# Three reorderings in a fused retention, mixture-of-experts and token-mixing kernel: weight loads, attention transposes, edge channel products

## The chip, the cores and the metric

The kernel runs on one core of one Trainium2 chip. The metric is the device time of one execution in microseconds (us). TensorE is called PE below, VectorE DVE, ScalarE ACT, GpSimd POOL, and SyncE, which issues nearly all transfers, SP.

## The reference

Eight batches of 576 tokens and 512 channels (8 heads of 64) pass three layers in float32.

```
scores = scale * q @ k.T ; ret = scores * gamma_h ** (i - j) for i >= j ; x = ret @ v          # retention
logits = x @ w_gate ; the best 2 of 4 experts, softmax over these two                         # gate
out   += w_e * (softmax(causal(scale * (x wq_e) @ (x wk_e).T)) @ (x wv_e) @ wo_e)             # per expert
theta  = x @ w_theta ; zr = x cos(theta) ; zi = x sin(theta)
u      = x + w_tok_r @ zr + w_tok_i @ zi                                                      # token mixing
result = u + max(u @ w_ch, 0)                                                                 # channel product
```

## The kernel before

Products whose operands need more than one PE pass are split into a high and a low part (`split`: ACT writes the high part, DVE the low one) and multiplied in three passes (`mm3`, lines 102 to 104).

**Start, 0 to 45 us.** The retention of batch 0 runs chunk by chunk (128 tokens) through `ret_step`: scores of a chunk (L144), a running state `pS` (L160, copied to SBUF by ACT as `S`, L163), values (L173 and L180), then `xt` (DVE), `xh` (ACT) and `xl` (POOL). `vp` (L129, POOL) scales V of a chunk and waits for that chunk's `kv` transfer. The projections of the experts need `w1`, 512 rows of 772 columns: Q and K in columns 0 to 512, V and the gate in 512 to 772. SP loads it as four blocks of rows, ahead of the chunks 1 to 3 of `kt` and `kv`, and each block is split whole into `WH` and `WL` (L435) behind chunk 0's `xt`. The first projection, `v0` (`proj_v`, L259), multiplies columns 512 to 772 of all four blocks. PE runs 50 matmuls on zeros before the first data and 40 more (`WARM2`) ahead of `v0`.

**Attention, 45 to 475 us.** The units (batch, pair of experts p, row tile m of 5) go through a loop in which the order on PE is written by hand (`manual_schedule`); the other engines' order is a scheduler's. Each batch has ten slots, table `SLOTS`; the last batch has `LAST`. A slot t issues: `at_scores` of unit t (L321; DVE takes the minimum, L324, and ACT the exponential `P`, L329), the projections that the table names, in slot 1 the products of V that are due ("O"), then `at_trans` of unit t-1 (L368: PE transposes `P`, DVE copies one expert's transpose to `PT`, ACT the other's, L373 and L375), and in five slots one `ret_step` of the next batch ("R1" to "R5"). Inside a `ret_step`, behind 12 groups of its values, `mid` issues the due products of V (`at_out`, L387), which read `PT`; what follows is the state of the next chunk, which writes `pS` again and so waits until ACT has copied `S`. All PSUM tiles of this phase but `pS` share one pool of 7 buffers, `w`.

**Mixing, 475 to 891 us.** Here the scheduler orders all engines. `mix(b, h)` multiplies 108 matmuls into the channel half h of batch b (L750), with the sines and products of `z_tile` (L599 to L608) as operands, which DVE and ACT prepare ahead. When a half is done, DVE adds x to it (L762; in batch 0, where x came in by transposes, it only copies, L764) and so frees the PSUM tiles `acc`; ACT and DVE or POOL split it to `uh`, `ul` (L765, L766). `channel(b, et)` multiplies four k tiles of `uh`, `ul` into one block of 128 output channels (2 column halves of 288, 12 matmuls each, 24 per block), of which k tiles 0 and 1 come from `mix(b, 0)`, 2 and 3 from `mix(b, 1)`. Four or five `token_tile`s for the coming batches (12 matmuls each, 512 wide; ACT L582, L584, DVE L585, L587) stand behind the halves. `x_put` (DVE L793, four SP transfers) writes x of later batches transposed to DRAM, `x_get` reads it back as `u`.

Of the kernel before, what the change touches and what calls it, by code (L numbers as in the profile page):

```python
# [10 lines left out]
F32 = mybir.dt.float32  # L11
# [5 lines left out]
OP = mybir.AluOpType  # L17
# [3 lines left out]
B, H, S, D = 8, 8, 576, 64  # L21
E, DM = 4, 512
C = 128
# [4 lines left out]
NW1 = 2 * 2 * 128 + NV  # L28
# [5 lines left out]
TH = [(0, 288), (288, 576)]  # L34
# [14 lines left out]
WARM2 = 40  # L49
# [13 lines left out]
def tile_kernel(ctx: ExitStack, tc: tile.TileContext, qk, kv, w1, wo, wot, wd, cst, out):  # L63
# [42 lines left out]
    def split(h, l, src):  # L106
        nc.scalar.activation(h, src, AF.Copy)  # L107
        MARK["split"] = nc.vector.tensor_sub(l, src, h)  # L108
# [318 lines left out]
    wst = []  # L427

    def load_w1(kt):
        st = w1s.tile([128, NW1], F32, name="wst", bufs=4)  # L430
        nc.sync.dma_start(st, w1[kt * 128:(kt + 1) * 128, :])
        wst.append(st)

    def split_w1(kt):
        split(WH[:, kt, :], WL[:, kt, :], wst[kt])  # L435

    for kt in range(4):
        load_w1(kt)
    for c in range(1, LDB):
        loads(0, c)  # L440
    with tc.issue_after(MARK["pool"].ins):
        nc.gpsimd.dma_start(cm, cst[:, o:o + 1088])
# [74 lines left out]
    for kt in range(4):  # L517
        with tc.issue_after(MARK["xt"].ins), tc.issue_after(MARK["xh" if kt > 1 else "S"].ins):
            split_w1(kt)
# [7 lines left out]
    scale()  # L527
    with tc.issue_after(MARK["sm"].ins):
        make_gt(2)
    ret_step(0, 1, (0, 2))  # L530
    for c in range(3, NCH):
        with tc.issue_after(MARK["xt"].ins):
            make_gt(c)
    w1s.release()
    ret_step(0, 2, (0, 3))
# [91 lines left out]
    outs = []  # L627
    for t in range(nu + 1):
        b, k = divmod(t, 10)
        if b < B - 1:  # L630
            more, between, after = *SLOTS[k], ""
        else:
            b = B - 1
            more, between, after = LAST[t - 10 * b]
        if t < nu:
            at_scores(units[t])
            work(b, more)
            if units[t][2] == NCH - 1:
                at_norm(*units[t][:2])
# [5 lines left out]
        if between == "O":  # L645
            for o in outs:
                at_out(*o)
            outs = []
        if t:
            at_trans(units[t - 1])  # L650
            ub, up, um = units[t - 1]
            if GROUPS[GRP[um]][-1] == um:
                outs.append((ub, up, GRP[um]))
        if b < B - 1:
            if between[:1] == "R":
                c = int(between[1])
                x = b + 1
                def mid():
                    for o in outs:
                        at_out(*o)  # L660
                    outs.clear()

                ret_step(x, c - 1, (x, c) if c < NCH else (x + 1, 0) if x + 1 < B else None, mid)
        else:
            work(b, between)
            for o in outs:
                at_out(*o)
            outs = []
# [42 lines left out]
    def mix(b, h):  # L711
# [7 lines left out]
        for i in tiles:  # L719
            if w == 0 or i != 4:  # L720
                z_tile(g, i, h)
# [36 lines left out]
        for d in range(2):  # L758
# [7 lines left out]
            (nc.vector if h else nc.gpsimd).tensor_sub(ul[:, k, :], u[:, k, :], uh[:, k, :])  # L766

    TAIL = {}
    EDGE = (0, B - 1)

    def channel(b, et):
# [3 lines left out]
        for j, (t0, t1) in enumerate(TH):  # L775
            spare = b in EDGE
            ps = ps2.tile([128, t1 - t0], F32, name=f"acc{et % 2}{j}" if spare else "w", bufs=1 if spare else 4,
                          padded_shape=[128, 512])
# [4 lines left out]
            if b == B - 1:  # L783
                nc.sync.dma_start(out[b, et, :, t0:t1], o)
        if b < B - 1:
            nc.sync.dma_start(out[b, et], u[:, et, :])
# [28 lines left out]
    for b in range(B):  # L815
# [20 lines left out]
        for et in range(4):  # L836
            channel(b, et)
            for x in q[2 * et:2 * et + 2] if not b else []:
                x_put(*x)
# [85 lines left out]
```

## Time and profile before

| | us |
|---|---|
| median of 3 runs (lowest, highest) | 894.57 (894.08, 895.03) |
| the profiled execution | 893.5 |
| its span, first to last instruction | 891.2 |
| PE busy in the span | 862.5 (97%) |
| DVE, ACT, POOL busy | 618.1, 465.8, 219.8 |

Busy time counts matmuls whose ends are modelled. In a row of a timeline the first number is the start, the second the length of the instruction or group, and the bracket at the end the idle time of that engine just before it and what released it. "issue" stands for idle time in which the engine waited for nothing that the profile shows.

### The profile page before, as it was taken

Reading aid. Unit: us, or ns where it says so; the run is one execution under the profiler, and the core shown is the slowest. Engines: PE = TensorE matmul, PEld = TensorE weight load, DVE = VectorE, ACT = ScalarE, POOL = GpSimd, SP = SyncE. Lnnn points to the kernel's source line nnn. Section 1 sums busy time; section 2 is a strip of 40 time slices with the busy share of each in tenths; the row PEclk is TensorE's granted clock in tenths of the full one; section 3 lists DMA queues with packets and bytes.
Section 4 is the critical chain, followed back from the end, with each engine's and each line's share of the span. In section 5 each row is a group of like instructions: output and inputs, shape, how many; then the busy total and the mean of one; then the engine's idle time right before and its main releaser. Section 6 shows DMA issues by size and latency. Waiting matters only on the chain.

```text
span 891.2 us, 25579 instructions
## 1 busy us (share of the span) xinstructions
PE 862.5 (97%) x10102; PEld 802.8 (90%) x10102; DVE 618.1 (69%) x1707; ACT 465.8 (52%) x1270; POOL 219.8 (25%) x268
## 2 busy tenths in 40 slices
PE   7899999999999999999999899999999999999998
PEld 6898989888898889988778899999999999999998
DVE  3387778878777886877767946966477764776632
ACT  3375666666666666666666613544245533445320
POOL 2325153443535444342300112010120101101010
PEclk9999999999999999999999999999999999999999
DMA  9758676676857667637795252334426124251311
GB/s 321 230 144 248 160 216 178 190 232 178 245 154 209 192 189 228 165 101 219 218 300 153 33 137 52 67 88 102 121 51 140 33 72 107 37 130 25 86 46 53
DMA packets 147126, 130.28 MB, mean 146 GB/s; under 512 B 84032, under 2 KB 122688, under 8 KB 147008
## 3 DMA queue, kind: packets, MB, share of 16 engines
q1 hardware_dynamic: 146864, 128.39, 52.3%
q8 instruction: 79, 1.29, 0.6%
q0 software_dynamic: 144, 0.28, 0.2%
q14 instruction: 39, 0.32, 0.1%
HBM read 78.03 MB, written 32.00 MB: 123 GB/s over the span
## 4 chain that ended last, share of the span: by engine, by line
PE 80%; DVE 11%; ACT 2%; DMA 2%; issue 2%; SPq 1%; POOL 0%; DVEq 0%; ACTq 0%; POOLq 0%
PE acc L750 21%; PE w L102 10%; PE w L104 10%; PE w L103 10%; PE w L321 5%; PE w L259 5%; PE w L387 5%; PE w L368 3%; PE pS L160 3%; PE w L750 2%; PE w L144 1%; DVE b L462 1%; DVE P L324 1%; PE w L180 1%; PE acc L102 1%
## 5 line engine op out<-in xcount | busy, mean ns | idle before, releaser
L750 PE MATMUL acc<-TK,zh 128*128 128x288 f32 (+2 forms) x896 | 155.9, 296 | 0.5 <-ACT ob L391 0.5
L750 PEld LDWEIGHTS acc<-TK,zh 128*128 128x128 f32 x896 | 131.9, 189 | 0.8 <-issue 0.6
L329 ACT ACTIVATE P<-P,st 128x128 f32<-128x128 f32 (+4 forms) x160 | 95.6, 598 | 43.1 <-DVE st L324 42.9
L750 PE MATMUL acc<-TK,zl 128*128 128x288 f32 (+1 forms) x448 | 95.8, 295 | 0.0
L766 POOL TENSOR_TENSOR ul<-u,uh 128x576 fp32r<-128x576 f32 x16 | 24.3, 1535 | 285.2 <-ACT uh L765 285.2
L324 DVE CUSTOM_DVE_ANT_0 P<-w,cm 128x128 f32<-128x128 f32 (+4 forms) x160 | 72.0, 477 | 10.4 <-PE w L321 10.1
L321 PE MATMUL w<-KK,U 128*64 128x288 f32 (+4 forms) x384 | 76.6, 327 | 0.3 <-issue 0.2
L102 PE MATMUL w<-xh,WH 128*128 128x288 f32 x256 | 75.9, 297 | 0.5 <-issue 0.5
L104 PE MATMUL w<-xh,WL 128*128 128x288 f32 x256 | 75.4, 295 | 0.0
L103 PE MATMUL w<-xl,WH 128*128 128x288 f32 x256 | 75.3, 294 | 0.0
L750 PEld LDWEIGHTS acc<-TK,zl 128*128 128x128 f32 x448 | 72.4, 189 | 0.0
L107 ACT ACTIVATE zh<-cs 128x512 fp32r<-128x512 f32 x64 | 40.3, 630 | 59.7 <-PE acc L750 43.6
L108 DVE TENSOR_TENSOR zl<-cs,zh 128x512 fp32r<-128x512 f32 x64 | 44.1, 689 | 37.3 <-ACT zh L107 36.7
L193 POOL TENSOR_TENSOR xl<-xt,xh 128x512 fp32r<-128x512 f32 (+1 forms) x40 | 48.7, 1219 | 82.5 <-ACT xh L192 74.6
L601 ACT ACTIVATE cs<-cs,quarter 128x256 f32<-128x256 f32 x72 | 36.4, 506 | 60.3 <-DVE cs L599 56.1
L604 DVE SCALAR_TENSOR_TENSOR cs<-cs,x 128x512 f32<-128x512 f32 x72 | 49.3, 687 | 19.9 <-ACT cs L602 19.1
L387 PE MATMUL w<-PT,V 128*64 128x192 f32 (+3 forms) x576 | 56.2, 325 | 6.4 <-DVE PT L373 4.9
L466 POOL TENSOR_TENSOR r<-r,ex 128x192 f32<-128x192 f32 (+1 forms) x51 | 29.4, 576 | 130.1 <-ACT hl L467 51.1
L321 PEld LDWEIGHTS w<-KK,U 128*128 128x128 f32 (+1 forms) x384 | 53.9, 171 | 6.8 <-issue 2.3
L368 PE MATMUL w<-ident,P 128*128 128x128 f32 (+2 forms) x480 | 59.0, 258 | 0.0
L387 PEld LDWEIGHTS w<-PT,V 128*64 128x64 f32 (+1 forms) x576 | 35.6, 135 | 24.3 <-DVE PT L373 6.5
L104 PE MATMUL w<-uh,CH 128*128 128x288 f32 x192 | 56.6, 295 | 0.0
(160 smaller groups left out, 2393.1 us busy)
## 6 DMA issues: line engine op xcount, KB each, us to landing
KK<-KN SPq DMA_DIRECT2D x128, 144.0 KB
kt<-qk SPq DMA_DIRECT2D x32, 512.0 KB
kv<-kv SPq DMA_DIRECT2D x32, 512.0 KB
raw<-wd SPq DMA_DIRECT2D x43, 192.0 KB
xd<-xb SPq DMA_DIRECT2D x126, 64.0 KB
out<-u SPq DMA_DIRECT2D x28, 288.0 KB
u<-xd SPq DMA_DIRECT2D x28, 288.0 KB
td<-hl SPq DMA_DIRECT2D x27, 192.0 KB
```

What stands on the lines that cost most here:

```text
L102: nc.tensor.matmul(ps, ah, bh, start=first, stop=False)
L103: nc.tensor.matmul(ps, ah, bl, start=False, stop=False)
L104: nc.tensor.matmul(ps, al, bh, start=False, stop=last)
L193: MARK["xl"] = nc.gpsimd.tensor_sub(xl[:, :, cs], xt, xh[:, :, cs])
L259: nc.tensor.matmul(ps[:R], x[:, kt, cs], W[:, kt, w0:w0 + NV], start=x is xh and W is WH and kt == 0, stop=x is xl and kt == 3)
L321: nc.tensor.matmul(ps[s][:R], U[:, s, rs], KK[:, s, x, j0:j1], start=x == 0, stop=x == 1)
L324: MARK["dve"] = nc.vector.tensor_tensor_reduce(Ps[s][:R, j0:j1], ps[s][:R], cm[:R, o + j0:o + j1], 1.0, st[:R, 0, s:s + 1] if i else 3.0e3 ...
L329: MARK["act"] = nc.scalar.activation(Ps[s][:R, :n], Ps[s][:R, :n], AF.Exp, bias=st[:R, last, s:s + 1], scale=-1.0, accum_out=SUM[p][:R, m, ...
L368: nc.tensor.transpose(tp[:w, j, :], Ps[s][:R, j * C:j * C + w], ident[:R, :R])
L387: nc.tensor.matmul(po[s * 64:s * 64 + 64, c0:], V[:ROWS[j], j, 2 * p + s, :], v, start=j == 0, stop=j == last, skip_group_check=True)
L604: nc.vector.scalar_tensor_tensor(z, cs, -1.0, x2[:, None, ds].to_broadcast([128, 2, 256]), op0=OP.mult, op1=OP.mult)
L750: nc.tensor.matmul(acc[d][j], A[:, dc], TK[:, kt, W, t0:t1], start=q == 0 and n == 0, stop=q == 8 and n == 2)
```

## The change

`w1` comes in two transfers: columns 512 to 772 (V and gate) of all four row blocks ahead of the chunks 1 to 3, columns 0 to 512 (Q and K) behind them. V's part is split in two pieces ahead of `v0`, Q's and K's in four pieces behind the retention step of chunk 2. `WARM2` goes from 40 to 10, and the load of the mask `cm` on POOL's queue goes behind the `vp` of a later chunk. In the attention loop `at_trans` of unit t-1 stands ahead of `at_scores` of unit t; in the slots with "R2" it goes into `mid` of that `ret_step`. In the first and the last batch `channel2` takes two blocks of output channels at once: the 24 matmuls on k tiles 0 and 1 of both, then the 24 on k tiles 2 and 3. In batch 0 `x_put` and in batch 1 the first half's `z_tile`s are issued behind the last `ul` of the half before (`MARK["u"]`).

```diff
@@ -46,7 +46,7 @@
          ("v0", "R3"), ("v1", ""), ("v2 k00", "R4"), ("q00", "R5"), ("v3 k01 v4 g", "")]
 PTV = (0,)
 WARM = 50
-WARM2 = 40
+WARM2 = 10
 WB = 7
 JOBS = (58, 75)
 
@@ -424,22 +424,21 @@
         R = ROWS[c]
         nc.vector.tensor_mul(gt[:, :, c * C:c * C + R], gt[:, :, :R], gf[:, :, c, None].to_broadcast([128, 4, R]))
 
-    wst = []
-
-    def load_w1(kt):
-        st = w1s.tile([128, NW1], F32, name="wst", bufs=4)
-        nc.sync.dma_start(st, w1[kt * 128:(kt + 1) * 128, :])
-        wst.append(st)
-
-    def split_w1(kt):
-        split(WH[:, kt, :], WL[:, kt, :], wst[kt])
-
-    for kt in range(4):
-        load_w1(kt)
+    wst = {}
+
+    def load_w1(a, z):
+        wst[a] = w1s.tile([128, 4, z - a], F32, name=f"wst{a}", bufs=1)
+        nc.sync.dma_start(wst[a], w1.rearrange("(k p) n -> p k n", p=128)[:, :, a:z])
+
+    def split_w1(a, k):
+        t = wst[a]
+        sl = slice(a, a + t.shape[2])
+        split(WH[:, k, sl], WL[:, k, sl], t[:, k])
+
+    load_w1(512, NW1)
     for c in range(1, LDB):
         loads(0, c)
-    with tc.issue_after(MARK["pool"].ins):
-        nc.gpsimd.dma_start(cm, cst[:, o:o + 1088])
+    load_w1(0, 512)
     nc.sync.dma_start(tie, cst[:, o + 1088:o + 1088 + E * E].rearrange("p (a b) -> p a b", a=E))
     nc.sync.dma_start(ident, cst[:, 0:128])
 
@@ -514,9 +513,9 @@
 
     ret_step(0, -1, (0, 0))
     ret_step(0, 0, None)
-    for kt in range(4):
-        with tc.issue_after(MARK["xt"].ins), tc.issue_after(MARK["xh" if kt > 1 else "S"].ins):
-            split_w1(kt)
+    for k in range(2):
+        with tc.issue_after(MARK["xt"].ins), tc.issue_after(MARK["xh" if k else "S"].ins):
+            split_w1(512, slice(2 * k, 2 * k + 2))
     with tc.issue_after(MARK["xl"].ins):
         scale()
     warm_up(WARM2)
@@ -525,14 +524,19 @@
         make_gt(1)
     ret_step(0, -1, (0, 1))
     scale()
+    with tc.issue_after(MARK["pool"].ins):
+        nc.gpsimd.dma_start(cm, cst[:, o:o + 1088])
     with tc.issue_after(MARK["sm"].ins):
         make_gt(2)
     ret_step(0, 1, (0, 2))
     for c in range(3, NCH):
         with tc.issue_after(MARK["xt"].ins):
             make_gt(c)
+    ret_step(0, 2, (0, 3))
+    for k in range(4):
+        with tc.issue_after(MARK["xt"].ins), tc.issue_after(MARK["xh"].ins):
+            split_w1(0, k)
     w1s.release()
-    ret_step(0, 2, (0, 3))
     work(-1, "v1")
     ret_step(0, 3, (0, 4))
     work(-1, "v2 k00")
@@ -625,6 +629,13 @@
     njobs = [len(x) for x in jobs]
     due = [(JOBS[0] - 2) / njobs[0], (JOBS[1] - JOBS[0]) / njobs[1]]
     outs = []
+
+    def trans(i):
+        at_trans(units[i])
+        ub, up, um = units[i]
+        if GROUPS[GRP[um]][-1] == um:
+            outs.append((ub, up, GRP[um]))
+
     for t in range(nu + 1):
         b, k = divmod(t, 10)
         if b < B - 1:
@@ -632,6 +643,10 @@
         else:
             b = B - 1
             more, between, after = LAST[t - 10 * b]
+        n0 = len(outs)
+        late = b < B - 1 and between == "R2"
+        if t and not late:
+            trans(t - 1)
         if t < nu:
             at_scores(units[t])
             work(b, more)
@@ -643,19 +658,17 @@
             atk.release()
             zp = pool("zp")
         if between == "O":
-            for o in outs:
+            for o in outs[:n0]:
                 at_out(*o)
-            outs = []
-        if t:
-            at_trans(units[t - 1])
-            ub, up, um = units[t - 1]
-            if GROUPS[GRP[um]][-1] == um:
-                outs.append((ub, up, GRP[um]))
+            del outs[:n0]
         if b < B - 1:
             if between[:1] == "R":
                 c = int(between[1])
                 x = b + 1
                 def mid():
+                    if late:
+                        trans(t - 1)
+                        return
                     for o in outs:
                         at_out(*o)
                     outs.clear()
@@ -718,7 +731,10 @@
         ks = []
         for i in tiles:
             if w == 0 or i != 4:
-                z_tile(g, i, h)
+                with ExitStack() as es:
+                    if b == 1 and not h:
+                        es.enter_context(tc.issue_after(MARK["u"].ins))
+                    z_tile(g, i, h)
             if w == 0 and i == 4:
                 TAIL[g, h] = ZT[g, 4, h]
             if i == 4:
@@ -763,27 +779,44 @@
                 else:
                     nc.vector.tensor_copy(u[:, k, t0:t1], acc[d][j])
             nc.scalar.activation(uh[:, k, :], u[:, k, :], AF.Copy)
-            (nc.vector if h else nc.gpsimd).tensor_sub(ul[:, k, :], u[:, k, :], uh[:, k, :])
+            MARK["u"] = (nc.vector if h else nc.gpsimd).tensor_sub(ul[:, k, :], u[:, k, :], uh[:, k, :])
 
     TAIL = {}
     EDGE = (0, B - 1)
+
+    def channel2(b, ets):
+        uh, ul = UT[b]
+        u = XU[b]
+        ps = {}
+        for h in range(2):
+            for et in ets:
+                es = slice(et * C, et * C + C)
+                for kt in (2 * h, 2 * h + 1):
+                    for j, (t0, t1) in enumerate(TH):
+                        if not kt:
+                            ps[et, j] = ps2.tile([128, t1 - t0], F32, name=f"acc{et % 2}{j}", bufs=1,
+                                                 padded_shape=[128, 512])
+                        mm3(ps[et, j], CH[:, kt, 0, es], CH[:, kt, 1, es], uh[:, kt, t0:t1], ul[:, kt, t0:t1],
+                            kt == 0, kt == 3)
+                for j, (t0, t1) in enumerate(TH if h else []):
+                    o = u[:, et, t0:t1]
+                    MARK["ch"] = nc.vector.scalar_tensor_tensor(o, ps[et, j], 0.0, o, op0=OP.max, op1=OP.add)
+                    if b == B - 1:
+                        nc.sync.dma_start(out[b, et, :, t0:t1], o)
+                if h and b < B - 1:
+                    nc.sync.dma_start(out[b, et], u[:, et, :])
 
     def channel(b, et):
         uh, ul = UT[b]
         u = XU[b]
         es = slice(et * C, et * C + C)
         for j, (t0, t1) in enumerate(TH):
-            spare = b in EDGE
-            ps = ps2.tile([128, t1 - t0], F32, name=f"acc{et % 2}{j}" if spare else "w", bufs=1 if spare else 4,
-                          padded_shape=[128, 512])
+            ps = ps2.tile([128, t1 - t0], F32, name="w", bufs=4, padded_shape=[128, 512])
             for kt in range(4):
                 mm3(ps, CH[:, kt, 0, es], CH[:, kt, 1, es], uh[:, kt, t0:t1], ul[:, kt, t0:t1], kt == 0, kt == 3)
             o = u[:, et, t0:t1]
             MARK["ch"] = nc.vector.scalar_tensor_tensor(o, ps, 0.0, o, op0=OP.max, op1=OP.add)
-            if b == B - 1:
-                nc.sync.dma_start(out[b, et, :, t0:t1], o)
-        if b < B - 1:
-            nc.sync.dma_start(out[b, et], u[:, et, :])
+        nc.sync.dma_start(out[b, et], u[:, et, :])
 
     XU = {}
 
@@ -833,10 +866,15 @@
                 x_put(*x)
         if 0 < b < B - 1:
             x_get(b + 1)
-        for et in range(4):
-            channel(b, et)
-            for x in q[2 * et:2 * et + 2] if not b else []:
-                x_put(*x)
+        if b not in EDGE:
+            for et in range(4):
+                channel(b, et)
+            continue
+        for i in range(2):
+            channel2(b, (2 * i, 2 * i + 1))
+            with tc.issue_after(MARK["u"].ins):
+                for x in q[4 * i:4 * i + 4] if not b else []:
+                    x_put(*x)
         if not b:
             x_get(1)
     ps2.release()
```

Where this puts instructions, at three places. The first is PE in slot 8 ("q00", "R5") of a batch: U and KK are Q and K of the unit, xh, xl, WH, WL belong to the projection q00, kt to the retention scores, PT and V to the products of V. Before:

```order
L321 MATMUL w<-KK,U 128x512 x4
L102 MATMUL w<-xh,WH 128x288
...
L368 MATMUL w<-ident,P 128x128 x6
L144 MATMUL w<-kt 64x64 x2
...
L387 MATMUL w<-PT,V 64x256 x4
L387 MATMUL w<-PT,V 64x128 x2
```

and with the change:

```order
L368 MATMUL w<-ident,P 128x128 x6
L321 MATMUL w<-KK,U 128x512 x4
L102 MATMUL w<-xh,WH 128x288
...
L144 MATMUL w<-kt 64x64 x2
...
L387 MATMUL w<-PT,V 64x256 x4
L387 MATMUL w<-PT,V 64x128 x2
```

The six transposes stood between the projection and the retention step whose middle reads their copies; now the scores and the projection lie between as well.

The second is DVE at the end of `mix(0, 1)`: cs, zh, zl, ztl belong to `z_tile`, x to the token tiles, the w read by COPY are the PSUM tiles of the mix. Before:

```order
L793 STREAM_TRANSPOSE xb<-x_8959 128x512
L604 SCALAR_TENSOR_TENSOR cs<-cs,x_8918 128x512
L604 SCALAR_TENSOR_TENSOR cs<-cs,x_8959 128x512
L108 TENSOR_TENSOR zl<-cs,zh 128x512
L599 TENSOR_SCALAR cs<-nr 128x256
L600 TENSOR_SCALAR cs<-nr 128x256
L108 TENSOR_TENSOR zl<-cs,zh 128x512
L764 COPY u<-w 128x256
```

and with the change:

```order
L608 SCALAR_TENSOR_TENSOR cs<-cs,x_8731 128x512
L108 TENSOR_TENSOR ztl<-cs,zth 64x256 x4
L780 COPY u<-w 128x256
L780 COPY u<-w 128x320
L780 COPY u<-w 128x256
L780 COPY u<-w 128x320
L782 TENSOR_TENSOR ul<-u,uh 128x576 x2
L826 STREAM_TRANSPOSE xb<-x_8731 128x512
```

The copies of u stood behind work for batch 1; now they follow the last operands of `mix(0, 1)` itself, and the transposes of x for batch 1 come after them.

The third is DVE at the end of `mix(1, 0)`: the acc are its PSUM tiles, k and nr belong to a token tile, u is batch 1's x, read back by `x_get`. Before:

```order
L604 SCALAR_TENSOR_TENSOR cs<-cs,x_8959 128x512
L108 TENSOR_TENSOR zl<-cs,zh 128x512
L762 TENSOR_TENSOR u<-acc_9537,u 128x288
L762 TENSOR_TENSOR u<-acc_9538,u 128x288
L762 TENSOR_TENSOR u<-acc_9539,u 128x288
```

and with the change:

```order
L589 TENSOR_SCALAR k<-k 128x512
L591 TENSOR_TENSOR nr<-k,w 128x512
L589 TENSOR_SCALAR k<-k 128x512
L591 TENSOR_TENSOR nr<-k,w 128x512
L778 TENSOR_TENSOR u<-acc_9507,u 128x288
L778 TENSOR_TENSOR u<-acc_9508,u 128x288
L778 TENSOR_TENSOR u<-acc_9509,u 128x288
```

The adds that free the tiles stood behind `z_tile` work; now they stand behind the k and nr of the fourth token tile, since PE's order has four token tiles (before: two) between `mix(1, 0)` and `mix(1, 1)`.

## Rows read from the trace of the kernel before

**Rows 1.** The page: busy time by engine, the chain by engine, one costly group.

```profile
PE 862.5 (97%) x10102; PEld 802.8 (90%) x10102; DVE 618.1 (69%) x1707; ACT 465.8 (52%) x1270; POOL 219.8 (25%) x268
...
L387 PE MATMUL w<-PT,V 128*64 128x192 f32 (+3 forms) x576 | 56.2, 325 | 6.4 <-DVE PT L373 4.9
```

**Rows 2.** Stretches of the span: us long, busy by engine (instructions), granted clock, DMA share, GB/s.

```profile
0.00:20.00 20.00, 15.77 (x342) 14.37 (x346) 8.01 (x11) 6.73 (x12) 6.24 (x15) 1.00 0.93 321
20.00:45.00 25.00, 20.25 (x460) 19.02 (x452) 7.75 (x17) 7.54 (x21) 8.36 (x9) 1.00 0.79 233
45.00:475.00 430.00, 417.19 (x6482) 373.96 (x6481) 333.36 (x1116) 280.97 (x886) 164.49 (x223) 1.00 0.68 196
```

**Rows 3.** What PE waited for: total us, times, longest.

```profile
PE pS L160 <- ACT S L163: 7.1, 11, 0.8
...
PE w L180 <- issue: 2.2, 2, 1.4
PE w L144 <- issue: 1.6, 1, 1.6
```

**Rows 4.** Timeline of PE, 9 to 18 us: start, us, operation, [idle before <-releaser].

```profile
16.00 0.65 PE L259 MATMUL w<-WH,xl 128*128 128x260 f32 x4
```

**Rows 5.** Timeline of DVE, 9 to 18 us.

```profile
11.06 4.66 DVE L108 TENSOR_TENSOR WL<-wst,WH 128x772 fp32r<-128x772 f32 x4
```

**Rows 6.** Timeline of POOL, 9 to 30 us.

```profile
16.56 1.04 POOL L129 TENSOR_TENSOR vp<-kv,gam 128x512 f32<-128x512 f32 x1 [2.53 <-DMA kv<-kv]
```

**Rows 7.** DMA of the first 50 us: one queue's packets, MB, share.

```profile
q8 instruction: 6, 0.10, 0.7%
```

**Rows 8.** Timeline of PE, 61 to 66 us (slot 4).

```profile
60.68 1.04 PE L368 MATMUL w<-ident,P 128*128 128x128 f32 x8
...
63.98 0.27 PE L160 MATMUL pS<-vp,kv 64*64 64x64 f32 x2 [0.70 <-ACT S L163]
```

**Rows 9.** Timeline of ACT, 61 to 66 us (slot 4).

```profile
62.99 0.56 ACT L373 COPY PT<-w 128x512 f32<-128x512 f32 x1
63.45 0.38 ACT L163 ACTIVATE S<-pS 128x256 f32<-128x256 f32 x1
```

**Rows 10.** Timeline of PE, 84 to 419 us (slot 8; last batch).

```profile
85.01 1.08 PE L387 MATMUL w<-PT,V 128*64 128x256 f32 x8 [0.43 <-DVE PT L373]
...
418.50 0.49 PE L387 MATMUL w<-PT,V 128*64 128x128 f32 x4 [1.41 <-DVE PT L373]
```

**Rows 11.** Timeline of PE and ACT, 228 to 234 us (slot 6).

```profile
230.33 0.64 PE L259 MATMUL w<-WH,xl 128*128 128x260 f32 x4
...
230.72 0.49 ACT L329 ACTIVATE P<-P,st 128x256 f32<-128x256 f32 x1
```

**Rows 12.** Timeline of PE and DVE, 503 to 516 us (first batch's channel product).

```profile
505.97 0.30 PE L102 MATMUL acc<-uh,CH 128*128 128x288 f32 x1
...
506.90 0.29 PE L103 MATMUL acc<-ul,CH 128*128 128x288 f32 x1
510.79 0.61 PE L102 MATMUL acc<-uh,CH 128*128 128x288 f32 x1 [3.60 <-ACT uh L765]
...
506.06 1.25 DVE L604 SCALAR_TENSOR_TENSOR cs<-cs,x 128x512 f32<-128x512 f32 x2
...
509.20 1.55 DVE L764 COPY u<-w 128x256 f32<-128x256 f32 x4
```

**Rows 13.** Stretch of the same place, PE alone: us, busy (instructions), granted clock.

```profile
510.25:513.70 3.45, 2.91 (x12) 0.51 0.00 0
```

**Rows 14.** Groups of 520 to 640 us: busy us, mean ns of one | idle before.

```profile
L762 DVE TENSOR_TENSOR u<-acc,u 128x288 f32<-128x288 f32 x16 | 6.4, 448 | 11.3 <-PE acc L750 11.3
...
L585 DVE TENSOR_SCALAR k<-k 128x512 f32<-128x512 f32 x9 | 6.3, 697 | 1.3 <-ACT k L584 1.2
L587 DVE TENSOR_TENSOR nr<-k,w 128x512 f32<-128x512 f32 x9 | 6.2, 683 | 0.2
...
L584 ACT ACTIVATE k<-w 128x512 f32<-128x512 f32 x9 | 5.3, 586 | 1.9 <-DVE nr L587 1.1 <-PE w L104 0.8
```

## The prediction

> **What bounds the kernel now.** I read the page first: PE is busy 862.5 us of the 891.2 us span [rows 1], so at most 28.7 us of it can be won by reordering, and every other engine has slack on average. Then the stretches: the first two show where PE idles at the start, 4.23 us (20.00 - 15.77) and 4.75 us, while the DMA engines are 93% and 79% busy; the attention phase idles 12.81 us (430.00 - 417.19) [rows 2]. From 475 to 891 us the idle time is one wait of 3.60 us near 510 us [rows 12] and the end. PE's list of waits gives the causes: copies of the state S (7.1 us in 11 waits) and 3.8 us of "issue" in three waits [rows 3]. The products of V wait 6.4 us, mostly for the DVE copy of a transpose [rows 1]. So the question for each part is which of these waits goes, and what is late next.
>
> **The weight loads.** `v0` ends at 16.65 us [rows 4]. What it waits for is DVE's four splits, 4.66 us from 11.06 on, 1.17 us for 772 columns [rows 5]. With the change the two pieces that `v0` needs have 2 x 260 columns, so 1.17 x 520/772 = 0.78 us each. The first runs from 11.06 us; the second waits for ACT, which does `xh` and a piece behind it: an ACT pass over 128x512 takes 0.59 us [rows 14], so 11.06 + 2 x 0.59 = 12.24 us, and DVE ends at 13.0. Behind that come two matmuls and the `xl` group of 0.65 us [rows 4], about 14.0 us, or up to 14.6 where POOL's `xl` is late; I take 14.35, a gain of 2.3 us. The next in line is chunk 1: POOL's `vp` began at 16.56 us, when `kv` had landed [rows 6]. Four blocks of 512 columns, 1.05 MB, no longer stand ahead of it in SP's queue; at 321 GB/s [rows 2] that is 3.3 us, so 13.3 us, and `vp` (1.04 us) ends at 14.3, just in time. Q's and K's part lands behind chunk 3. Its four splits cost ACT and DVE about 0.8 us each, in a stretch where both are under a third busy (7.54 and 7.75 of 25 us [rows 2]), some microseconds ahead of the first projection that reads it; costed at nothing, and 4 x 0.78 = 3.1 us if that cover is gone. The mask's later load is hidden by the 20 us until its first reader. Thirty warm-up matmuls less save nothing by themselves, since `v0` waits anyway.
>
> Between 20 and 45 us the waits that nothing in the profile explains remain. They stand 256 PE instructions apart, counted in PE's order, and a queue named "instruction" moves 6 packets of 16 KB (0.10 MB) in the first 50 us [rows 7], while the DMA engines are full. I read them as PE waiting for its next instructions, a time that follows the instruction count and not the weights, and keep them: -2.3 us, between 0 (they grow by what is won) and -4.5 (the two of 2.2 us [rows 3] go as well). The Trainium skill says in "Runtime: NRT & Kernel Launch", section "Instruction fetch mechanics", that crossing such a block is mostly hidden; by that the three waits would be late data. The rows speak against it, as no transfer or engine releases them. What it would give is the fourth rival.
>
> **Transposes ahead of the scores.** Three kinds of wait are touched. (a) Slot 4: PE waits 0.70 us for S [rows 8], because ACT copies a `PT` for 0.56 us ahead of S, 0.38 us [rows 9]; seven batches have it. As matmul ends are modelled past the next start, the loss from start to start is some 0.15 us more, 0.85 in all. With the change the 8 transposes, 1.04 us [rows 8], stand in this very gap and the copies of their results behind S. The exponentials of the slot's own scores then come about a microsecond later against the step, so I leave 0.3 us: (0.85 - 0.3) x 7 = 3.9 us. (b) Slots 5 and 8 and the last batch: 17 waits, 6.4 us together [rows 1], the first in slot 8 and the longest, 1.41 us, in the last batch [rows 10], plus 0.12 us each for the same reason, 8.4 us. The copies now have the scores and a projection more, 2 us and longer, so these go: 8.4 us. (c) The new wait is of the transposes for their own exponentials. Most slots have a `ret_step` or a long projection between scores and the next transposes. The tight ones are slots 1 and 6: in slot 6 the projection `v1` issues its last group at 230.33 us, about 0.5 us long, while ACT begins the second exponential only at 230.72 and takes 0.49 us [rows 11]: the end is 0.4 us late for the first matmul that would follow, and the first two transposes cover a part. I take 0.3 us a batch for both slots together, 2.1 us in seven. Sum 3.9 + 8.4 - 2.1 = 10.2 us gained. Bounds: 15 (PE's whole idle time with the added 0.12 to 0.15 a wait, no new one) and 4 (every slot without a `ret_step`, five of ten, waits 0.2 us).
>
> **Channel product, first batch.** PE runs 8 matmuls and waits 3.60 us for `uh`, since DVE does `z_tile` work first and the four copies only at 509.20, 1.55 us [rows 12]. Right behind, the granted clock is 0.51, the lower of its two levels (1.2 GHz), for 12 matmuls that take 2.91 us [rows 13]; at full clock 7 starts take 0.93 us, 0.133 each [rows 12]. So 12 x (0.24 - 0.133) = 1.3 us more. With the change the copies follow the mix at once; half of them and one ACT pass give the first `uh` 0.78 + 0.67 = 1.45 us behind it (0.59 x 576/512), and 24 matmuls on the first half cover 24 x 0.133 = 3.2 us. Both losses go: -4.9 us, between -3.6 and -5.2.
>
> **What is late next.** The delayed `x_put` and `z_tile` push batch 1's x back. The order on PE answers with four token tiles instead of two between the halves of `mix(1)`, and DVE does the adds that free `acc` behind the fourth tile's nr. From PE's last token matmul to the first free tile it takes ACT 0.59, DVE 0.70 + 0.68 and one add 0.45 [rows 14], 2.4 us with nothing for PE to do: I take +2.5 us. The low end is 0, if DVE's passes are shorter there; the high end +3.8, if the clock falls as it did behind the 3.6 us wait, for 1.3 us more.
>
> **Last batch.** PE has no wait between its mix and its last products, so nothing is won; both halves of the last blocks end together, so one more DVE pass of about 0.45 us stands at the end at worst: +0.2, between 0 and +0.5.
>
> **Sum.** -2.3 - 10.2 - 4.9 + 2.5 + 0.2 = -14.7 us. The profiled execution took 893.5 us, so 878.8; it is 1.07 us below the median of the runs, so **879.9 us** against 894.57.
>
> **Rivals.**
> 1. The transposes' waits move rather than go: PE waits for the exponentials as long as it waited for the copies, as slot 6 shows it can [rows 11]. Against it: most slots have 2 us of work between. Then -2.3 - 4.9 + 2.5 + 0.2 = -4.5, **890.1 us**.
> 2. The edges give less: the start is held by instructions and full DMA engines [rows 2, 7] (0 instead of -2.3), and the wait in batch 1 lowers the clock (+1.3). For it: both have happened in this trace. -11.1, **883.5 us**. That a granted clock falls behind a long PE wait is also what the Trainium skill's page "TensorE: Matmul & The Clock Gate" says; the trace agrees in the one place that shows it, 0.51 [rows 13].
> 3. Slower: one mechanism, the wait of L368 for ACT. ACT is 65% busy in the attention phase (280.97 of 430 [rows 2]) and does copies and conversions between exponentials; if transposes come before these in 70 units and wait w each, the change loses 70w. The rest of it gains 14.7 + 2.1 = 16.8 us, so it is slower from w = 0.24 us on average; at 0.4 us, +28 - 16.8 = +11.2, **905.8 us**. Against it: the waits that I find are in two slots of ten.
> 4. The "issue" waits are late data and go with the earlier chunks: 3.8 us [rows 3] more, **876.1 us**.
>
> **How the numbers follow.** Forecast 0.55, rival 1 0.14, rival 2 0.20, rival 3 0.05, rival 4 0.06. The forecast's own spread by its bounds is about 5 us to either side; with rival 2 and 4 inside and rival 1 at the edge the range is 873 to 890.5. Some 0.2%, 1.8 us, is what a measurement of this kernel can tell from no change. Faster by more: 0.92, all but rival 3 and a poor case of rival 1; the same 0.03; slower 0.05.
>
> **What would show it.** Right: `v0` ends near 14.3 us; the waits of L387 for `PT` all but gone, those of L160 in slot 4 under 0.4 us; new waits at L368 of 2 to 3 us in all, in slots 1 and 6; no wait at 506 to 511 us and a clock of 1.00 there; one new wait of 2 to 3 us in the middle of `mix(1)`, for DVE. Wrong: over 10 us of waits at L368 (rivals 1 and 3), "issue" waits that vanish (4) or grow (2), or a wait in batch 1 far from 2.5 us.

## The result and the profile after

The changed kernel takes 899.74 us (median of 11 runs, 894.88 to 907.27); the kernel before, timed with it, 894.53 us (11 runs, 892.22 to 895.59). The ratio is 1.0071 with a 95% interval of 1.0052 to 1.0089: slower by 0.7%, where 879.9 us was forecast, outside the range. The spread is news of its own: 12.4 us instead of 3.4 (in the later rounds the kernel before spread by 5.5 to 9.0 us). It goes with the granted clock, TensorE's share of its full 2.4 GHz, of which the mean over each execution is on record: 0.998 in the changed kernel's fastest run and 0.986 in its slowest, with a median of 0.991, where the kernel before has 0.996 in the later rounds. Executions over 1.5% above the fastest of their kernel are left out of medians and ratios, here two of run 9's twelve, of 907.3 and 907.57 us.

The profiled execution took 899.74 us, its span is 897.5 us, 6.3 us longer than before's. Its page and its stretches (us long, busy us of each engine with instructions, granted clock, DMA share, GB/s), to be read against [rows 1, 2]:

```profile
PE 869.5 (97%) x10072; PEld 805.5 (90%) x10072; DVE 624.4 (70%) x1709; ACT 464.2 (52%) x1272; POOL 221.3 (25%) x268
```

```profile
0.00:20.00 20.00, 16.54 (x335) 15.18 (x337) 6.25 (x9) 4.95 (x10) 6.04 (x15) 0.91 0.94 319
20.00:45.00 25.00, 20.75 (x429) 19.89 (x426) 11.35 (x22) 9.05 (x25) 8.59 (x8) 0.93 0.77 235
45.00:85.00 40.00, 36.36 (x609) 32.93 (x611) 27.83 (x93) 23.11 (x76) 11.31 (x15) 0.91 0.54 150
85.00:475.00 390.00, 380.28 (x5840) 337.79 (x5829) 305.44 (x1010) 251.48 (x797) 154.22 (x208) 1.00 0.68 198
475.00:500.00 25.00, 24.51 (x183) 22.51 (x182) 20.41 (x48) 18.27 (x41) 1.32 (x1) 1.00 0.41 144
500.00:520.00 20.00, 20.00 (x152) 19.77 (x151) 12.64 (x26) 6.54 (x14) 2.18 (x2) 1.00 0.07 14
520.00:870.00 350.00, 346.98 (x2376) 333.55 (x2376) 234.00 (x492) 149.18 (x310) 35.18 (x19) 1.00 0.37 85
```

PE's idle time, 28.0 us (897.5 - 869.5), is only 0.7 us less than before's 28.7, so what the change won in waits it lost again in new ones. PE is as busy as before by share, but it is busy for 7.0 us longer, and most of the cause stands in the first three rows: a granted clock of 0.91 to 0.93, where before showed 1.00 up to 475 us [rows 2]. Four stretches make it up (PE alone):

```profile
13.84:17.25 3.41, 3.39 (x40) 0.50 1.02 401
24.08:27.49 3.41, 3.41 (x121) 0.50 0.69 220
51.39:54.80 3.41, 3.41 (x15) 0.50 0.50 114
71.87:75.28 3.41, 3.41 (x91) 0.50 0.42 92
```

At half clock a stretch of 3.41 us costs at most 1.7 us, the four at most 6.8; before's trace has one, near 510 us [rows 13]. The channel product of batch 0, 500 to 520 us, has lost its wait and its low clock [rows 12, 13], as forecast.

What PE waited for (us in total, times, longest), against [rows 3]:

```profile
PE pS L160 <- ACT S L163: 7.1, 11, 0.8
PE acc L766 <- DVE u L778: 3.0, 1, 3.0
PE pS L160 <- issue: 2.4, 1, 2.4
PE w L368 <- ACT P L329: 2.1, 2, 1.7
...
PE w L180 <- issue: 1.0, 1, 1.0
...
PE w L321 <- DVE ML L108: 1.0, 1, 1.0
PE w L368 <- DMA wost<-wot: 1.0, 1, 1.0
PE w L104 <- DVE oll L108: 0.8, 1, 0.8
```

The waits of L387 for `PT`, 6.4 us before [rows 1], are not among the larger ones any more. Those for S still make 7.1 us in 11 waits, though the transposes were moved for them too. New are the waits of L368 for an exponential, the one for the adds in batch 1, and the last three rows: they stand in the last batch, where 2.6 us of waits for `PT` went and these 2.8 us came.

By place, from the first scores (L321) and the first product of the mixing: the start takes 44.0 us (44.1 before), the attention phase 437.8 (430.3), the rest of the span 415.8 (416.8). So 7.4 us were lost in the attention phase; from the first scores of batch 0 to those of batch 1 it takes 56.5 us instead of 49.6, from there to the last batch 315.2 instead of 314.5. (In the changed kernel transposes of the batch before lie ahead of these scores, which shifts such marks by under 1 us.) The timeline of PE in batch 0 has three waits:

```profile
50.10 0.93 PE L368 MATMUL w<-ident,P 128*128 128x128 f32 x4 [1.67 <-ACT P L329]
...
51.69 0.44 PE L102 MATMUL w<-xh,WH 128*128 128x288 f32 x1
52.41 0.44 PE L102 MATMUL w<-xh,WH 128*128 128x288 f32 x1
...
55.08 0.30 PE L102 MATMUL w<-xh,WH 128*128 128x288 f32 x1
55.48 0.30 PE L102 MATMUL w<-xh,WH 128*128 128x288 f32 x1
...
65.22 0.27 PE L160 MATMUL pS<-vp,kv 64*64 64x64 f32 x2 [0.81 <-ACT S L163]
...
69.54 0.21 PE L180 MATMUL w<-kt,S 64*64 64x64 f32 x1 [1.05 <-issue]
```

From one L102 to the next, three matmuls, it takes 0.72 us behind the first wait and 0.40 at full clock.

### The profile page after: what moved, and what is told of

The parts are those of the page before. It is cut to its first block, busy times and chain, and to the rows that moved or that the text cites. A ratio compares the mean times of both kernels' runs of the same rounds, so it can differ in the third digit from the quotient of the medians.

```text
span 897.5 us, 25593 instructions
## 1 busy us (share of the span) xinstructions
PE 869.5 (97%) x10072; PEld 805.5 (90%) x10072; DVE 624.4 (70%) x1709; ACT 464.2 (52%) x1272; POOL 221.3 (25%) x268
## 4 chain that ended last, share of the span: by engine, by line
PE 85%; DVE 7%; ACT 3%; DMA 3%; issue 2%; POOL 1%; SPq 0%; POOLq 0%; DVEq 0%; ACTq 0%
PE acc L766 23%; PE w L102 9%; PE w L103 9%; PE w L104 9%; PE w L259 5%; PE w L321 5%; PE w L368 5%; PE w L387 5%; PE w L766 3%; PE pS L160 3%; PE w L144 3%; PE w L180 1%; PE acc L102 1%; PE acc L104 1%; PE acc L103 1%
## 5 line engine op out<-in xcount | busy, mean ns | idle before, releaser
L321 PE MATMUL w<-KK,U 128*64 128x288 f32 (+4 forms) x384 | 77.1, 328 | 1.1 <-DVE ML L108 1.0
L102 PE MATMUL w<-xh,WH 128*128 128x288 f32 x256 | 76.6, 299 | 0.0
L104 PE MATMUL w<-xh,WL 128*128 128x288 f32 x256 | 75.9, 297 | 0.0
L108 DVE TENSOR_TENSOR zl<-cs,zh 128x512 fp32r<-128x512 f32 x64 | 44.1, 689 | 37.5 <-ACT zh L107 37.1
L368 PE MATMUL w<-ident,P 128*128 128x128 f32 (+2 forms) x480 | 64.9, 265 | 3.9 <-ACT P L329 2.1
L368 PEld LDWEIGHTS w<-ident,P 128*128 128x128 f32 (+2 forms) x480 | 45.7, 138 | 16.2 <-ACT P L329 6.7
L321 PEld LDWEIGHTS w<-KK,U 128*128 128x128 f32 (+1 forms) x384 | 54.4, 171 | 4.8 <-DVE ML L108 1.3
L104 PE MATMUL w<-uh,CH 128*128 128x288 f32 x192 | 56.6, 295 | 0.0
L103 PE MATMUL w<-ul,CH 128*128 128x288 f32 x192 | 56.5, 294 | 0.0
```

Of the source, the lines that this page charges most:

```text
L102: nc.tensor.matmul(ps, ah, bh, start=first, stop=False)
L103: nc.tensor.matmul(ps, ah, bl, start=False, stop=False)
L104: nc.tensor.matmul(ps, al, bh, start=False, stop=last)
L321: nc.tensor.matmul(ps[s][:R], U[:, s, rs], KK[:, s, x, j0:j1], start=x == 0, stop=x == 1)
L368: nc.tensor.transpose(tp[:w, j, :], Ps[s][:R, j * C:j * C + w], ident[:R, :R])
```

## The experiments

The theory with which I went to the chip (theory 1): the loss is made of stretches at the lower clock, which the waits of the single parts set off. Its rival (theory 2): the order in the slots costs the time by itself. I took the change apart, mended what each part did badly, and put the parts together again. Every kernel was timed in five rounds against the kernel before; its median there was 893.8 to 894.3 us. Runs 5 to 8 were made on another chip than the rest, so between these groups the differences from the kernel before are the better measure. Each kernel has one profile.

**1. The weight part alone**: the first four pieces of the diff (`w1`, splits, `cm`, `WARM2 = 10`).

> The kernel before with the weight part alone (two transfers, WARM2 10, cm later). Theory 1 (the loss is made of stretches at the lower clock in the first 75 us, set off by PE waits that each part adds): the stretch from 13.8 us, behind the shortened warm-up, and one behind a wait for instructions stay, so the first scores (L321) start at 43 to 45 us as before, 44.1; nothing later changes; 893 to 897 us, with a wider spread of runs than before. Theory 2 (the loss is the slot order's alone): the weights win what the prediction said, first scores near 41.8 us, 892.3 us.

893.01 us, ratio 0.9989 (0.9978 to 1.0). In its profile the first scores come at 44.3 us, as theory 1 expected; the wider spread did not come (892.10 to 894.16 us, against 891.76 to 900.78 of the kernel before in the same rounds).

**2. The same with the long warm-up.**

```diff
-WARM2 = 10
+WARM2 = 40
```

> As a_weights, with WARM2 at 40 again. Theory 1: no stretch at the lower clock near 13.8 us; v0 ends near 14.3 us instead of 15.4, and the time is 1 to 2 us below a_weights. Theory 2: the 30 matmuls end before v0 can start, so the same as a_weights within 0.5 us.

892.85 us, ratio 0.9977 (0.9959 to 0.9996). The two medians are 0.2 us apart, so here the number of warm-up matmuls shows no effect; theory 1 expected 1 to 2 us. The traces differ, though. With 10 (first) there are two stretches at 0.50 in the first 45 us, and the scores of chunk 1 come at 15.38 us; with 40 (second) there is none, and they come at 14.76, 1.8 us before the 16.58 of before. `v0` ends at 14.83 us, near the forecast's 14.35. One trace each does not settle the start: of the seven kernels whose start is unchanged (before and runs 3 to 8), five have a stretch at 0.50 at 15.7 to 17.2 us too, and their first scores come anywhere between 42.4 and 44.8 us.

```profile
14.74:18.15 3.41, 3.41 (x52) 0.50 1.03 396
24.98:28.39 3.41, 3.17 (x73) 0.50 0.73 201
```

```profile
14.19 0.64 PE L259 MATMUL w<-WH,xl 128*128 128x260 f32 x4
14.76 1.15 PE L144 MATMUL w<-kt 64*64 64x64 f32 x32
```

**3. The transposes alone** (the three pieces of the diff in the loop over t).

> The kernel before with the transposes alone ahead of the scores. Theory 1: the wait of 1.7 us at L368 in slot 2 of batch 0 is there, with a stretch at the lower clock behind it, and the wait for S stands in slot 4 as before, at the step's start: batch 0 is 3 to 6 us longer, each later batch within 0.5 us of before: 896 to 901 us. Theory 2: the same loss but with no part of the clock: over 3 us of new PE waits in batch 0.

897.93 us, ratio 1.0036 (1.0016 to 1.0056): this part is slower, not 10 us faster. Batch 0 is 4.8 us longer, as theory 1 expected; the later ones differ by -1.9 to +1.5 us, 0.5 together. The trace has the wait in slot 2 and 0.50 behind it, and a second thing: behind `mix(0)` the old channel product now waits 4.85 us instead of 3.60, with 6.8 us at the lower clock.

```profile
48.57 0.44 PE L368 MATMUL w<-ident,P 128*128 128x128 f32 x2 [1.67 <-ACT P L329]
```

```profile
50.00:53.41 3.41, 3.41 (x16) 0.50 0.47 111
514.21:521.04 6.83, 5.19 (x21) 0.50 0.13 22
```

**4. The channel part alone** (the last three pieces).

> The kernel before with the channel products alone. Both theories: the 3.6 us wait and the low clock at 510 us go (-4.9), one wait of 3.0 us in mix(1) comes (measured with all parts), 1 to 2 us below before: 892.5 to 893.5 us.

892.66 us, ratio 0.9983 (0.9966 to 1.0). The wait in `mix(1)` is there, and in this run the clock falls behind it, which the changed kernel's trace does not show:

```profile
544.99 1.07 PE L753 MATMUL acc<-TK,zth 128*128 128x288 f32 x4 [3.02 <-DVE u L765]
```

```profile
545.84:549.25 3.41, 3.41 (x17) 0.50 0.07 12
```

**5. The transposes, slot 2 of batch 0 as before.** There no product of V is due yet, so nothing lies on PE between the scores of slot 1 and their transposes, and DVE, which still has the gate, `U`, `PT` and `KN` to do, comes to the minimum of these scores late.

```diff
-        if t and not late:
+        if t and not late and t != 2:
             trans(t - 1)
...
+        if t == 2:
+            trans(t - 1)
```

> The transposes alone, but in slot 2 of batch 0 (t = 2) they stay behind the scores. Theory 1 (batch 0's loss is its 1.7 us wait at L368 in slot 2 and the lower clock behind it, about 1.3 us): both go, first batch of attention 3 us shorter than in b_transposes, time near 895. Rival (the loss is spread over slots that wait for PSUM buffers and exponentials): the time stays within 1 us of b_transposes, 897.9.

895.03 us, ratio 1.0012 (0.9998 to 1.0026); 2.9 us below run 3 (+1.1 against the kernel before instead of +3.6). Theory 1 holds for this part. From the first scores to those of batch 1 it takes 50.6 us instead of 54.4, at a clock of 1.00. But with the slip gone the transposes still win nothing, and there theory 2 has its share.

**6. Slot 4's transposes divided.**

```diff
+        if late:
+            trans(t - 1, (0,))
...
                     if late:
-                        trans(t - 1)
+                        trans(t - 1, (1,))
                         return
```

`at_trans` takes the experts to transpose as an argument; the rest is run 5.

> As b_old_slot2, and in slot 4 the transposes of one expert stand ahead of the retention step and only the other's in its middle. Theory (the wait for S was moved from the step's middle to its start, since the transposes no longer cover the copy of S that ACT makes behind xh): the wait at the start shrinks from 0.75 to 0.3 us in each of seven batches and none comes back in the middle: 3 us below b_old_slot2. Rival (ACT is late by a fixed time, wherever PE asks): the wait of 0.7 us comes back in the middle, no gain.

889.64 us, ratio 0.9955 (0.9938 to 0.9973); 5.4 us below run 5, and the interval lies below 1 for the first time among the runs of the transposes. The waits of six batches, 93 to 405 us, in run 5 and in run 6:

```profile
PE pS L160 <- ACT S L163: 4.8, 7, 0.8
```

```profile
PE pS L160 <- ACT S L163: 2.2, 7, 0.4
```

No wait of this kind appears in the middle of the step instead, and a batch is 0.2 to 1.1 us shorter than in run 5, all seven together 4.5 us. The waits for S, with batch 0's, are 3.1 us shorter, as the 3 us that were expected; where the rest of the gain comes from was not tried by itself.

**7. The channel part, `x_put` not held back.**

```diff
-            with tc.issue_after(MARK["u"].ins):
-                for x in q[4 * i:4 * i + 4] if not b else []:
-                    x_put(*x)
+            for x in q[4 * i:4 * i + 4] if not b else []:
+                x_put(*x)
```

> The channel part alone, without holding x_put behind the last ul. Theory (the wait in mix(1) comes from x_put's delay, which makes batch 1's x late, so that four token tiles and their nr stand ahead of the adds): no wait at the 545 us place, adds at once, the channel wait of batch 0 still gone or under 0.7 us; 3 to 4.5 us below before, 890 to 891.5. Rival (z_tile's delay is to blame): the wait of 3.0 us stays, the same time as c_channel, 892.7.

888.83 us (6 runs), ratio 0.9946 (0.9927 to 0.9965), 5.1 us below the kernel before and more than expected. Both places are without idle time and at full clock:

```profile
500.00:520.00 20.00, 20.00 (x151) 1.00 0.35 88
535.00:560.00 25.00, 25.00 (x156) 1.00 0.30 58
```

**8. The channel part, `z_tile` not held back** (the `issue_after` in `mix` taken out, `x_put` held).

> The channel part alone, with x_put held back but z_tile free. Theory (x_put's delay): the 3.0 us wait in mix(1) stays; besides, the copies of u come late again behind z_tile, so a part of the 3.6 us wait comes back: 893 to 896 us. Rival (z_tile's delay): the wait in mix(1) goes, 890 to 891 us.

893.81 us, ratio 1.0 (0.9985 to 1.0015). 0.69 and 0.40 us of the old wait come back and the wait in `mix(1)` stays, 2.43 us: it is `x_put`'s delay that makes it.

```profile
511.81 0.40 PE L102 MATMUL acc<-uh,CH 128*128 128x288 f32 x1 [0.69 <-ACT uh L766]
...
550.13 1.16 PE L751 MATMUL acc<-TK,zth 128*128 128x288 f32 x4 [2.43 <-DVE u L763]
```

**9. Weights and transposes together** (runs 1 and 3). The single parts add up to about 895 us (-1.3, +3.6, -1.7), the whole takes 899.7; so two of them disturb each other.

> Weight part and transposes together, without the channel part. Adding the single results (-1.3 and +3.6 on 894.3) gives 896.6. Theory (the two disturb each other in the first 75 us: fewer matmuls move the waits for instructions into batch 0 of the attention, where the transposes have just added waits, so the clock falls there a second time): 899 to 902 us, with a wait for instructions near 70 us and the lower clock behind it. Rival (no interplay of these two; what is more than the sum comes from the channel part): 896 to 897.5 us.

899.91 us (10 runs, 893.65 to 904.61), ratio 1.0059 (1.0035 to 1.0083), as the theory expected. The spread is here too. The profiled execution has this in batch 0:

```profile
71.36 0.26 PE L180 MATMUL w<-kt,S 64*64 64x64 f32 x1 [3.42 <-issue]
```

```profile
70.53:77.35 6.82, 5.99 (x55) 0.50 0.39 115
```

**10. All of the change, slot 2 of batch 0 as before** (the edit of run 5).

> All of the change, with slot 2 of batch 0 in the old order. Theory (slot 2's wait starts the chain of low clock in batch 0): 3 to 6 us below the changed kernel's 899.7, so 894 to 897. Rival (S and the instructions lower the clock by themselves): less than 2 us below.

897.22 us, ratio 1.0039 (1.0025 to 1.0053): 2.5 us below the changed kernel, between the two expectations. The wait without a releaser at the place of run 9's, here 2.33 us, comes without slot 2's wait as well.

**11. All of the change with `WARM2 = 40`.**

> All of the change with WARM2 at 40. Theory (the shortened warm-up costs the low clock at v0 and moves the instruction waits by 60 PE instructions into batch 0): 3 to 5 us below the changed kernel, 895 to 897. Rival (warm-up matmuls have no effect beyond v0, as the pair of weight runs says): within 1.5 us of 899.7.

894.81 us (892.57 to 898.84), ratio 1.0011 (0.9997 to 1.0025): 4.9 us below the changed kernel, from the 30 matmuls that "save nothing by themselves". In the traces, whose spans differ by 5.0 us, 2.3 us stand before the first scores, which single profiles do not settle (run 2), and 3.6 us in batch 0, while the rest takes 0.9 us more; there is no "issue" wait in batch 0 any more. Slot 2's wait is still there, but without a stretch at the lower clock behind it:

```profile
47.81 0.93 PE L368 MATMUL w<-ident,P 128*128 128x128 f32 x4 [1.67 <-ACT P L329]
```

```profile
45.00:60.00 15.00, 13.28 (x197) 1.00 0.46 111
```

The stretch of 60 to 80 us here and in the changed kernel:

```profile
60.00:80.00 20.00, 18.90 (x444) 1.00 0.64 200
```

```profile
60.00:80.00 20.00, 18.14 (x449) 0.91 0.52 159
```

**12. All of the change, mended**: `WARM2 = 40` and the edits of runs 5, 6 and 7.

> All of the change with WARM2 at 40, slot 2 of batch 0 in the old order, slot 4's transposes divided, and x_put not held back. Adding what the single runs gave (-1.5 weights, -4.3 transposes with both mends, -5.1 channel, and 1 to 2 us more since the channel wait that those transposes lengthened is gone): 881 to 885 us. Rival (gains do not add, as the changed kernel's losses did not): 886 to 889 us.

881.52 us (4 runs, 880.78 to 882.42), ratio 0.9858 (0.9845 to 0.9871), 12.3 us below the kernel before and 18 below the changed one. Its stretches around the old losses:

```profile
0.00:20.00 20.00, 15.40 (x360) 14.34 (x362) 6.26 (x9) 4.95 (x10) 6.05 (x15) 1.00 0.94 320
...
45.00:85.00 40.00, 39.66 (x784) 35.85 (x783) 32.44 (x99) 26.10 (x84) 17.13 (x23) 1.00 0.65 180
...
520.00:860.00 340.00, 340.00 (x2329) 327.08 (x2329) 221.31 (x462) 143.76 (x295) 34.95 (x19) 1.00 0.34 77
```

With the slips mended the parts do add: 881 to 885 us was expected. That this is near the forecast's 879.9 us is luck: in its trace the start is 2.2, the attention phase 4.4 and the rest 4.7 us shorter than before's, where 2.3, 10.2 and 2.2 were forecast.

## Why the prediction was wrong

**The weight loads** (forecast -2.3, bounds 0 and -4.5): right within its bounds. Alone they give about -1 to -2 us (runs 1 and 2). What the prediction did not have is a wait of PE for a later chunk's `vp`, 0.5 to 1.3 us at 35 to 38 us, in all seven traces with this part and in none of the seven without it.

**The instruction waits, which I "keep"**: the reading fits, the conclusion was not right. Before's trace has four such waits, not three; the fourth, at L102, is 0.5 us. Counting all of PE's records (matmuls, weight loads and its waits for semaphores), the "issue" waits of 0.2 us and more, 42 in the fourteen traces, stand at record 705 or a multiple of 256 behind it, whatever instruction that is. The traces also have the time of each 16 KB packet on the queue "instruction": 40 of the 42 waits end 1.2 to 1.7 us behind the end of such a packet. The Trainium skill calls such crossings mostly hidden ("Runtime: NRT & Kernel Launch", section "Instruction fetch mechanics"). Over the whole span the traces agree, with one to six waits at some 80 such places; in the first 40 us they do not, where the kernel before has four in a row, 0.5 to 1.6 us each. So the waits do follow the instruction count. Then taking 60 records out (30 matmuls with their weight loads) moves the program against these marks, a cost that I put at nothing: I never asked what would come to lie there. In the changed kernel record 2241 falls 272 records behind the start of slot 4's retention step in batch 0, whose products are small and quick, and PE waits 1.05 to 3.42 us there (the changed kernel, runs 9 and 10), with the lower clock behind it. With 40 warm-up matmuls it falls 60 records earlier in the step, and there is no wait (runs 11 and 12). The packets fit: in the changed kernel the one before this wait ends at 68.18 us, 0.3 us before PE begins to wait; in run 11 it ends at 61.12 us, 2.9 us before PE comes to that record. The exchange of the warm-up shows the effect, 4.9 us in the whole change; that it is the place in the step that decides is read from these five traces, not tried by itself. The same edit does nothing between runs 1 and 2, where the transposes are in their old places.

**Transposes ahead of the scores** (forecast -10.2; alone +3.6): this step failed, in two of its three terms, and most in (c). For the sizes below I took each interval of PE from one start to the next, less the median for its kind of matmul in the kernel before, put it down to the matmul behind it, and compared run 3, the transposes alone, with the kernel before.
(a) The 8 transposes were to "stand in this very gap": they do, and the wait in the middle of slot 4's step is gone. But they had also stood between the previous copy of S and the step's first product (L160), which overwrites `pS`. ACT does `xh` and a copy of `ob` ahead of that S, and in the changed kernel PE now waits for it at the step's start. ACT's timeline and PE's at this place:

```profile
224.25 0.63 ACT L192 ACTIVATE xh<-xt 128x512 fp32r<-128x512 f32 x1 [1.74 <-DVE xt L190]
224.78 0.35 ACT L391 COPY ob<-w 128x256 f32<-128x256 f32 x1
225.03 0.39 ACT L163 ACTIVATE S<-pS 128x256 f32<-128x256 f32 x1
```

```profile
225.47 0.27 PE L160 MATMUL pS<-vp,kv 64*64 64x64 f32 x2 [0.75 <-ACT S L163]
```

So 0.55 us won per batch became up to 0.1 lost. Run 6, which covers both ends with half of the transposes each, shows that 3.1 us of these waits could be won, and 5.4 us with what came along.
(b) The 8.4 us of `PT` waits were sized right: the products of V lose 8.4 us less, 5.5 in the seven batches and 2.9 in the last.
(c) "I take 0.3 us a batch" for new waits, 2.1 us in all, was too little; about 12 us came. In the seven batches L321, L368 and the projections behind them lose 8.4 us more, 3.6 of them in batch 0 and 0.8 in each other one, in pieces of 0.1 to 0.3 us, of which the list of waits shows only some (for exponentials, and for PSUM tiles that DVE's `PT` copies hold: `L259 <- DVE PT`, 0.5 us in three waits in run 5). The last batch, which I gave no new wait, loses 4 us more at L368, L321 and L104. The lower bound, 0.2 us in five slots of a batch, had the size of a steady batch. That the list of the changed kernel has just 2.1 us for L368 is luck: it is one wait of 1.67 us, between slots 1 and 2 of batch 0, and one of 0.40 in the last batch, none of this length behind slots 1 and 6 of the other batches. I had judged the tight slots by a steady batch, and in batch 0 no product of V is due in slot 1: that wait costs 2.5 to 2.9 us with the clock behind it (run 5).

**Channel product, first batch** (-4.9): right; no wait, clock 1.00. **What is late next** (+2.5): right in its place, its cause and nearly its size, 3.02 us; runs 7 and 8 show `x_put`'s delay as the cause. Where the clock falls behind it, as in run 4, little of the gain is left: -1.7 us alone, -2.2 forecast with the last batch's +0.2.

**The rivals.** Rival 1, that the transposes' waits move rather than go, is nearest to what happened in this step: it has 0 us for the transposes, and run 5, without slot 2's slip, gives +1.1. But they moved to the copy of S, to scores and projections, and not to the exponentials alone. Rival 3 had the sign but not the size: L368 waits 2.1 us in all by the list, and by the count of (c) it is some 0.1 us for each of 70 units at L321, L368 and the projections together, not 0.24. Rival 2 said that instructions and clock hold the edges, and the clock it took for one place came in four. Rival 4, "issue" waits that go with earlier chunks, did not happen: they stay at their marks. None said that waits of two parts would meet in one place.

What stays open: which waits set off the lower clock in a given execution. The spread of 12 us goes with the mean granted clock of the runs (0.998 to 0.986). The waits of 1.05, 2.33 and 3.42 us at the same record, with stretches at 0.50 behind them, vary enough to take part in it, but each kernel has one profile, which does not show the spread.

## What to carry to other kernels

Work that is moved out of a place was covering something there: ask what each of its two ends hid, not only the wait that you want it to fill. Check the first round of a loop by itself, since the slot that is safe in the steady state may stand empty there. Where a small wait sets off a stretch at the lower clock, it can cost more than its length (2.5 to 2.9 us for the 1.67 us of slot 2): remove the wait. And test a removal of filler work with the whole change in place: 30 matmuls less cost nothing beside the old order (runs 1 and 2) and 4.9 us beside the new one (run 11).

## What the runs showed of the hardware

PE's "issue" waits of 0.2 us and more came only at fixed distances of 256 of PE's records, in all fourteen traces; they cost 0.2 to 3.4 us each, and 40 of 42 ended 1.2 to 1.7 us behind the end of a 16 KB packet on the queue "instruction". Which of the marks show a wait was changed by taking out instructions far ahead of them, but it also differs between traces with the same start: at the first of these marks, 705, it is 2.06 us in run 8, 0.37 us in run 4 and under 0.2 us in run 3.

The granted clock fell to 0.50 not only behind waits of 3 us and more but also behind one of 1.67 us (slot 2, run 3) and behind the pair of 0.81 and 1.05 us in the changed kernel, while other waits of that length passed without it (1.67 us in run 11, whose clock stayed 1.00 there). Behind the wait of 3.02 us in `mix(1)` it fell in run 4 and did not in the changed kernel.
